# Retention attention into a mixture of experts: first row numbers one step later, places woven, the second expert's rows asked for first

## The chip, the cores and the metric

One core of a Trainium2 chip runs the whole kernel as one program. The metric is the device time of one execution in microseconds (us); a kernel's time is the median of its runs. Engines are called as in the profile: PE (matrix products), DVE and ACT (elementwise work), POOL (elementwise work and indirect DMAs), SP (issues most DMAs).

## The reference

```python
# attention: B=4, H=8, S=768, D=64, blocks of 64 tokens, state kv per (batch, head)
for b in range(12):
    intra = einsum(einsum(qb, kb) * Dmask, vb)
    inter = einsum(qb * lam_pow, kv)
    out[:, :, block b] = intra + inter
    kv = lam_block * kv + einsum(kb * rev_pow, vb)
x = out transposed to [3072, 512]
# mixture of experts, E=8, hidden 1024, each token goes to one expert
e_idx = argmax(x @ w_gate); gate_w = softmax(x @ w_gate)[e_idx]
eom = sigmoid(x @ w_output_gate)
for e in range(8):
    out[mask] = gate_w * eom[:, e] * (relu(x[mask] @ w1[e]) @ w2[e])
```

Only the rows that chose an expert go through its weights, so the kernel has to sort 3072 rows by expert while it runs.

## The kernel before, in words

**Stage 1** computes x in 24 tiles of 128 tokens (tile n is time chunk n // 4 of batch n % 4, all heads). A software pipeline (L1248 to L1334) runs steps s = -2 to 21. A step works on several tiles: `stage_a` transposes keys and queries of tile s+2 on PE into the banks `pk`, `pq` (ACT copies them out); `stage_c1` starts the output `po` of tile s from the state; `stage_b` makes the scores `ps` of tile s+1 and `stage_b2` multiplies them by the decay on DVE (`at`, L407, two halves); `stage_c` finishes `po` of tile s, copies it as `xT`, and adds the new keys to the state (PE `pst`, DVE L464); `stage_d2` (L521) transposes `xT` of an earlier tile on DVE (L530) and stores its rows to DRAM (`x_d`, SP DMA at L532). Tiles 20 to 23 are stored after the loop, two at a time.

PE writes to eight PSUM banks, handed out strictly in turn by `bank`; a step stands when its next bank is still being read.

**Routing.** For each four tiles, PE makes logits (L499, L509), `route_choose` (L542) picks the expert of each row, and `route_place` (L586) gives each row its place in that expert's list: a few small matmuls into a rank bank `pr` (`ranks`) and 15 small DVE operations (L637 to L632, ending in a reciprocal). From tile 8 on they keep their scratch in the rank bank itself, so that bank comes free with the last of the 15. POOL then scatters a record per row into a table in DRAM (`place_scatter`, L677, one indirect DMA per tile). `weave` runs pending small operations between the large ones of a step; `late` holds `ranks` for the next step; `held` holds places for step 21 (`RES + 5`, with `RES0` = 12, `RES` = 16, `LAST` = 20).

At step 12 the expert that leads is picked, to be computed first. At the end of step 15 POOL loads the first numbers of its list (`load_rows`, L831), `row_index` (L861) turns them into row numbers on DVE (L866, four times L871), and POOL gathers x rows from DRAM (`gather`, L897), one indirect DMA for 32 rows of each quarter: the table `work` places these gathers (`row(b)`) and the record scatters (`rec`) at three points of each step. `x_turn` (L908) transposes gathered rows on DVE, `x_hi` (ACT, L928) and `x_lo` (DVE, L932) split them into a high and a low part for the matrix products, which use three products for each pair (L85 to L87). Weights come in pieces of 1 MB over SP (`load_piece`) and are split the same way (ACT L132, DVE L141 and L146).

**Between the loop and the experts** the last tiles are finished while PE already computes the first 192 rows of the first expert with pending `units` (`fill`, `settle`). There `sort_rest` orders the other seven experts, `expert_regs` (L734) reads their numbers into registers of SP and POOL, `load_outs0` loads three tables of places where the results go, `load_rows(1)` the list of the second expert.

**The experts** run in the loop over p (L1437): for each of eight columns fc, `up` makes 12 matmuls into `ph`, ACT makes `hhi` (L1006) and DVE `hlo` (L1007); then the second product, `down`. `next_rows` (L1020) first does a `pace`, a POOL copy of one element of `hhi` that holds POOL until ACT has made it, then gathers for a later expert.

Of the kernel before, what the change touches and what calls it, by code (L numbers as in the profile page):

```python
# [9 lines left out]
F32 = mybir.dt.float32  # L10
# [13 lines left out]
def kernel(  # L24
# [496 lines left out]
    def stage_d2(n, count=1):  # L521
        if count == 1:
            xn = slot(f"xn_{n}")
        else:
            xn = pool.tile([P, 8 * P], F32, tag="wide", bufs=4, name=f"xn_{n}")
        for i in range(count):

            src = live.pop(n + i)["xT"].rearrange("p (g b r) -> p b g r", g=NPAIR, b=4)
            dst = xn[:, i * DM : (i + 1) * DM].rearrange("p (b g c) -> p b g c", b=4, g=NPAIR)
            nc.vector.transpose(dst, src)  # L530
            weave()
        nc.sync.dma_start(  # L532
            x_d[n * P : (n + count) * P, :].rearrange("(i p) m -> p i m", p=P),
            xn[:, 0 : count * DM].rearrange("p (i m) -> p i m", m=DM),
        )
# [196 lines left out]
        )  # L732

    def expert_regs(p, in_i, n):  # L734
        _, regs = nc.values_load_multi_w_load_instructions(
            in_i[0:1, 0:n], engines=[mybir.EngineType.SP, mybir.EngineType.Pool], min_val=0, max_val=E - 1
        )
        expert.update(zip(range(p, p + n), regs))

# [168 lines left out]
    def x_turn(p, i):  # L908
        if p >= E or i >= KT[p]:
            return  # L910
        w = P * (min(4, NB[p] - 4 * i) if p else (4, 2, 4, 1)[i])
        if (p, i // 2) not in ys:
            ys[(p, i // 2)] = pool.tile([P, 8 * P], F32, tag="wide", bufs=4, name=f"y_{p}_{i // 2}")
        nc.vector.transpose(ys[(p, i // 2)][:, 512 * (i % 2) : 512 * (i % 2) + w], xg[(p, i)][:, 0:w])  # L914
# [288 lines left out]
    def settle():  # L1203
        while acts:
            acts.pop(0)()

    def fill(count):
        for _ in range(min(count, len(units))):
            mm, act = units.pop(0)
            mm()  # L1210
            if act:
                acts.append(act)

    with tc.manual_schedule():
# [11 lines left out]
        def row(b):  # L1226
            return lambda: gather(0, b, b + 1, RES0 * P)

        def rec():
# [6 lines left out]
            RES0 + 1: ([], [], [rec]),  # L1236
            RES0 + 2: ([], [rec], [rec]),
            RES0 + 3: ([], [rec], [lambda: load_rows(0, 0, 2, nc.gpsimd)]),
            RES: ([], [], [row(0)]),
            RES + 1: ([], [row(1)], [rec]),  # L1240
            RES + 2: ([rec], [], [rec]),
            RES + 3: ([row(2)], [], [rec]),
            RES + 4: ([row(3)], [], [row(4)]),
            RES + 5: ([row(5)], [], [rec]),
# [3 lines left out]
        for s in range(-2, NTILE - 2):  # L1248
            if s >= 0:
                load_up_to(s + AHEAD - (4 <= s <= RES), 2 if s <= RES else 1)  # L1250
            for i in range(3):
                if s == RES + (2, 4, 5)[i]:
                    load_piece(i)
            if s == -2:
                decay_table()
            if s == 0:
                stage_b(1)
                stage_b2(1)
            rest = stage_a(s + 2)
            if late and s != RES + 5:  # L1260
                late.pop(0)()
            if s >= 1 and s % B == 0:
                logits(s - B, B)
            for f in rest:
                f()
            if s >= 0:
                stage_c1(s)
            stage_a2(s + 2)
            if s == RES + 4:
                stage_q(s + 2)  # L1270
            if s + 1 >= 0 and s != 0:
                stage_b(s + 1)
            if s == RES + 5:
                late.pop(0)()
                seen = rank_counts("plater")
            n = s - 1
            if s >= 1 and s % B == 0:
                logit_rows(s - B)
            if n >= 0 and n % B == B - 1:
                choice = route_choose(n + 1 - B, n + 1)  # L1280
                ranking = route_place(n + 1 - B, n + 1)
                if s != RES + 4:
                    at_once(choice)
                    pace(uncounted[-1][0][0:1, 0, 0:1])
                per_turn[0] = 3 if n >= RES - 1 else 2
            if s + 1 >= 0 and s != 0:
                stage_b2(s + 1)
            stage_k(s + 2)
            if s == RES0 + 1:
                weave(len(later))  # L1290
            if s == RES0 + 2:
                expert_regs(0, order_i, 1)
            if s == RES:
                row_index(0)
            if s == RES + 5:
                for f in held:
                    f()
                keep_places(seen, LATE)
            gap_work(s, "end")
            if s == RES + 1:  # L1300
                weave(len(later))
            if s == RES + 4:
                at_once(choice[:-1])
            if s == RES + 5:
                x_turn(0, 0)
            if 0 <= n < LAST:
                stage_d2(n)
            if s == 0:
                later.extend(inter_tables())
                routing_tables()  # L1310
                order_tables()
            if s == 1:
                weave(len(later))
            if s == 2:
                blank_rows()
            if s >= 0:
                stage_c(s)
            if s == RES + 4:
                choice[-1]()
            if ranking and s == RES + 4:  # L1320
                late.append(ranking[0])
                held = ranking[1:]
                ranking = []
            if ranking and s not in (RES0, RES):
                late.append(ranking[0])
                later.extend(ranking[1:])
                ranking = []
            if ranking:
                first_steps = pick_first() if s == RES0 else []
                for f in first_steps[:1] + ranking:  # L1330
                    f()
                later.extend(first_steps[1:])
                ranking = []
            if s < RES0 - 2:  # L1334
                place_scatter(1)
# [4 lines left out]
        stage_c1(n - 1)  # L1340
        stage_b(n)
        stage_b2(n)
        place_scatter(B)
        load_rows(0, 1, 3, nc.gpsimd)
        x_turn(0, 1)
# [41 lines left out]
            split_hi(2, j)  # L1387
        row_index(0, 1)
        gather(0, 6, 11, LAST * P)
        stage_d2(LAST, 2)  # L1390
        stage_d2(n - 1, 2)
        split_late()
        sort_rest(counts)
        load_outs0()
        expert_regs(1, order_i[:, 1:E], E - 1)
        load_rows(1)
        load_piece(4)
        for h in range(2):
            split_hi(3, 2 * h)
            split_hi(3, 2 * h + 1)  # L1400
            fill(8)
            split_lo2(2, h)
            settle()
        for h in range(2):
            split_lo2(3, h)
            fill(2)
        settle()
        row_index(1)
        gather(1, 0, 4)
        load_piece(5)  # L1410
        x_turn(0, 2)
        x_turn(0, 3)
# [24 lines left out]
        for p in range(E):  # L1437
# [5 lines left out]
            for fc in range(NFC):  # L1443
                if p == 0:
                    up(p, fc, 1)
                    next_rows(1, 6 + fc, 7 + fc, hts[(p, fc)][0][0:1, FIRST : FIRST + 1].bitcast(F32))
                    if fc >= 4:
                        next_split(4, (fc - 4,))
                    if fc >= 5:
                        for f in work[:2]:  # L1450
                            f()
                        work = work[2:]
                else:
                    up(p, fc)
                    next_split(4 * p + 2, (fc,))

                    if fc == 1 and p in TURNED:
                        out_index(p)
                    if fc == 3 and p == 2:
                        count_over()  # L1460
                    if fc >= 4:
                        for f in work[: (fc - 2) // 2]:
                            f()
                        work = work[(fc - 2) // 2 :]
                if fc == 3 and p in TURNED:
                    down_banks(p)
                if p > 0 and fc < 4:
                    b = 4 * 2 if p - 1 in TURNED else 3 * 2 if p > 1 else 2 * 2
                    n = (14 - b + 3) // 4
                    next_rows(p + 1, b + n * fc, b + n * fc + n, hts[(p, fc)][0][0:1, 0:1].bitcast(F32))  # L1470
                if fc == 0:
                    load_outs(p + 1)
                    load_rows(p + 2)
                if p - 1 in TURNED:
                    if fc == 2:
                        fetch_turned(p - 1)
                    if fc >= 5:
                        send_turned(p - 1, fc - 5)
# [127 lines left out]
```

## Time and profile before

| | us |
|---|---|
| median of 3 runs | 435.49 |
| lowest, highest | 432.88, 436.21 |
| the profiled execution | 438.91 |
| its span in the trace | 437.3 |

| engine | busy us | share of the span |
|---|---|---|
| PE | 409.5 | 94% |
| PE weight loads | 372.0 | 85% |
| DVE | 285.1 | 65% |
| POOL | 233.7 | 53% |
| ACT | 189.2 | 43% |

The profile is of one execution, 438.91 us by its own clock and 437.3 us from its first instruction to its last; the shares are averages over stages that differ. PE's clock is granted at one of two levels, 1.2 and 2.4 GHz; the profile shows it as a share of the higher one, 0.98 over the whole span.

### The profile page before, as it was taken

What the parts mean: (1) busy time and instruction counts of PE and PEld (TensorE: products, weight loads), DVE (VectorE), ACT (ScalarE), POOL (GpSimd) and SP (SyncE); (2) the same over time, 40 slices, a digit from 0 to 9 for tenths busy, and PEclk for the clock granted to TensorE, in tenths of its full rate; (3) what the DMA queues carried; (4) which work ended last, traced back from release to release, by engine and by line L of the source; (5) the groups of instructions that cost most, each with busy time, mean ns of one, the idle gap of its engine ahead of it and who ended that gap; (6) DMA issues with size and microseconds to landing.
All of it is one profiled execution on the core that took longest, in us unless ns stands there. A gap on an engine that the chain in (4) does not pass through costs nothing.

```text
span 437.3 us, 10557 instructions
## 1 busy us (share of the span) xinstructions
PE 409.5 (94%) x3869; PEld 372.0 (85%) x3869; DVE 285.1 (65%) x810; ACT 189.2 (43%) x460; POOL 233.7 (53%) x294
## 2 busy tenths in 40 slices
PE   7898999979979997998999999999999999999993
PEld 4787877768859786897999899999999989989983
DVE  3658696756678744773964985796785774874610
ACT  5666655544657113432602533532642552542400
POOL 4176678765854666574468086375476446311011
PEclk9999999996999998999999999999999999999997
DMA  6899988779932491444357455974964886361001
GB/s 169 205 245 250 259 210 225 179 195 233 327 122 85 131 340 43 133 169 133 118 202 238 154 210 163 290 230 148 291 223 122 241 284 214 127 214 47 2 25 49
DMA packets 96077, 79.20 MB, mean 181 GB/s; under 512 B 59452, under 2 KB 71744, under 8 KB 96016
## 3 DMA queue, kind: packets, MB, share of 16 engines
q1 hardware_dynamic: 89696, 65.54, 50.6%
q0 software_dynamic: 6176, 12.90, 9.6%
q8 instruction: 32, 0.52, 0.5%
q14 instruction: 29, 0.24, 0.2%
q10 hardware_dynamic: 144, 0.00, 0.0%
HBM read 62.25 MB, written 16.55 MB: 180 GB/s over the span
## 4 chain that ended last, share of the span: by engine, by line
PE 73%; issue 6%; DMA 6%; DVE 6%; POOL 5%; SPq 2%; ACT 1%; another core or an unknown queue 0%; POOLq 0%; DVEq 0%
PE ph_None L87 8%; PE ph_None L86 8%; PE ph_None L85 8%; PE py L87 5%; PE pyr L86 5%; PE py L86 5%; PE py L85 5%; PE pyr L85 5%; PE pyr L87 5%; PE ps L398 2%; PE ph L86 2%; PE po L439 2%; PE ph L87 2%; PE ph L85 2%; DMA raw<-in_moe_w_dram 1%
## 5 line engine op out<-in xcount | busy, mean ns | idle before, releaser
L897 POOL DMA_INDIRECT xg<-x_d,rows x100 | 110.9, 1109 | 71.6 <-issue 45.2
L1006 ACT ACTIVATE hhi<-ph_None 128x400 fp32r<-128x400 f32 (+4 forms) x56 | 28.0, 501 | 120.0 <-PE ph_None L87 94.5
L86 PE MATMUL ph_None<-xlo,whi 128*128 128x400 f32 (+4 forms) x224 | 76.2, 340 | 1.4 <-issue 1.4
L87 PE MATMUL ph_None<-xhi,wlo 128*128 128x400 f32 (+4 forms) x224 | 76.2, 340 | 1.1 <-issue 1.1
L85 PE MATMUL ph_None<-xhi,whi 128*128 128x400 f32 (+4 forms) x224 | 76.2, 340 | 0.0
L141 DVE TENSOR_TENSOR wlo<-raw,whi 128x512 fp32r<-128x512 f32 x112 | 74.4, 685 | 0.5 <-ACT whi L132 0.5
L132 ACT CAST whi<-raw 128x512 fp32r<-128x512 f32 x128 | 74.6, 616 | 0.0
L1007 DVE SCALAR_TENSOR_TENSOR hlo<-ph_None,hhi 128x400 fp32r<-128x400 f32 (+4 forms) x56 | 31.7, 566 | 47.4 <-ACT hhi L1006 26.9
L87 PE MATMUL py<-hhi,wlo 128*128 128x400 f32 (+2 forms) x128 | 44.6, 349 | 0.1
L86 PE MATMUL py<-hlo,whi 128*128 128x400 f32 (+2 forms) x128 | 44.5, 348 | 0.1
L85 PE MATMUL py<-hhi,whi 128*128 128x400 f32 (+2 forms) x128 | 44.5, 348 | 0.0
L407 DVE TENSOR_TENSOR at<-ps,decay 128x512 f32<-128x512 f32 x48 | 31.1, 682 | 19.5 <-PE ps L398 18.7
L87 PEld LDWEIGHTS ph_None<-xhi,wlo 128*128 128x128 f32 x224 | 42.0, 188 | 1.9 <-issue 1.6
L85 PEld LDWEIGHTS ph_None<-xhi,whi 128*128 128x128 f32 x224 | 42.0, 188 | 1.5 <-issue 1.1
L86 PEld LDWEIGHTS ph_None<-xlo,whi 128*128 128x128 f32 x224 | 42.0, 188 | 0.7 <-issue 0.4
L1123 POOL DMA_INDIRECT out_dram<-yn,table x12 | 12.6, 1053 | 53.3 <-DVE yn L1187 36.0
L343 ACT COPY qT<-pq 64x256 f32<-64x256 f32 x96 | 37.5, 391 | 3.8 <-PE pq L339 2.5
L86 PE MATMUL pyr<-wlo,hhi 128*128 128x512 f32 (+2 forms) x96 | 37.8, 394 | 0.4 <-issue 0.4
L85 PE MATMUL pyr<-whi,hhi 128*128 128x512 f32 (+2 forms) x96 | 37.5, 390 | 0.0
L87 PE MATMUL pyr<-whi,hlo 128*128 128x512 f32 (+2 forms) x96 | 37.4, 390 | 0.0
L677 POOL DMA_INDIRECT tab_d<-rec,idx x24 | 26.5, 1105 | 13.5 <-issue 5.3
L928 ACT CAST xhi<-y 128x256 fp32r<-128x256 f32 (+3 forms) x64 | 19.5, 357 | 31.6 <-DVE y L914 27.2
(214 smaller groups left out, 787.2 us busy)
## 6 DMA issues: line engine op xcount, KB each, us to landing
raw<-in_moe_w_dram SPq DMA_DIRECT2D x32, 1024.0 KB
qkv<-in_k_dram SPq DMA_DIRECT2D x40, 128.0 KB
qkv<-in_q_dram SPq DMA_DIRECT2D x40, 128.0 KB
qkv<-in_v_dram SPq DMA_DIRECT2D x20, 256.0 KB
x_d<-xn SPq DMA_DIRECT2D x20, 256.0 KB
yd<-yo SPq DMA_DIRECT2D x12, 256.0 KB
yr<-yd SPq DMA_DIRECT2D x48, 64.0 KB
xg<-x_d,rows POOLq DMA_INDIRECT x100
```

Of the source, the lines that this page charges most:

```text
L85: nc.tensor.matmul(ps, a[0], b[0], start=first, stop=False)
L86: nc.tensor.matmul(ps, a[0], b[1], start=False, stop=False)
L87: nc.tensor.matmul(ps, a[1], b[0], start=False, stop=last)
L132: nc.scalar.copy(out=hi, in_=src)
L141: eng.tensor_tensor(out=lo, in0=src, in1=hi.bitcast(F32), op=ALU.subtract)
L343: copies = [lambda r=r, view=view, src=src: nc.scalar.copy(out=view(qT[r]), in_=src) for r, view, src in query_parts(pq)]
L407: nc.vector.tensor_tensor(out=at, in0=ps.rearrange("p (g t) -> p g t", g=NPAIR), in1=dec[:, j], op=ALU.mult)
L677: nc.gpsimd.indirect_dma_start(out=tab_d, out_offset=bass.IndirectOffsetOnAxis(ap=idx, axis=0), in_=rec, in_offset=None, bounds_check=P * ...
L897: nc.gpsimd.indirect_dma_start(out=xg[(p, i)][:, m * P : (m + 1) * P], out_offset=None, in_=x_q[0 : 4 * rows], in_offset=bass.IndirectOffs ...
L928: nc.scalar.copy(out=hi, in_=src)
L1006: nc.scalar.activation(out=hi[:, r], in_=ph[:, r], func=AF.Relu)
L1007: nc.vector.scalar_tensor_tensor(out=lo[:, r], in0=ph[:, r], scalar=0.0, in1=hi[:, r].bitcast(F32), op0=ALU.max, op1=ALU.subtract,)
```

## The change

It has seven parts, none of which changes what is computed.

1. The first row numbers (`row_index(0)`) are made at the end of step 17, not 16. The gathers `row(0)` and `row(1)` are a step later, and record scatters are put in their places; one scatter that was inside the loop is now behind it.
2. The places of tiles 12 to 15 are no longer made in one go at the end of step 16: `ranks` goes to step 17, and the 15 DVE operations are woven through it, six in `stage_a2`, three behind each half of `at`, the last three behind the row numbers.
3. At step 21, tile 20 is transposed and stored inside the loop (one SP DMA more); `x_turn(0, 0)` stands ahead of the places of that step, of which six operations stay there and nine go behind the loop's last `at`. After the loop tile 21 is stored alone, tiles 22 and 23 together.
4. The second expert's number is read alone and its list and weight piece 4 are asked for at once; the result tables and the other six numbers follow.
5. Numbers of later experts are read by SP alone, without POOL's registers.
6. The second expert's row numbers and first four gathers stand half a weight split earlier.
7. At p = 1 the gathers for expert 2 are spread: one for each fc (fc 6 has two), each behind its own `pace`, where before fc 0 to 3 had three each.

`live.pop` became `live[...]`, which issues nothing.

```diff
     def expert_regs(p, in_i, n):
+        engines = [mybir.EngineType.SP] + ([] if p else [mybir.EngineType.Pool])
         _, regs = nc.values_load_multi_w_load_instructions(
-            in_i[0:1, 0:n], engines=[mybir.EngineType.SP, mybir.EngineType.Pool], min_val=0, max_val=E - 1
+            in_i[0:1, 0:n], engines=engines, min_val=0, max_val=E - 1
...
-            RES: ([], [], [row(0)]),
-            RES + 1: ([], [row(1)], [rec]),
-            RES + 2: ([rec], [], [rec]),
+            RES + 1: ([], [], [row(0)]),
+            RES + 2: ([row(1)], [rec], [rec]),
...
+            if s == RES + 5:
+                stage_d2(LAST)
             if s + 1 >= 0 and s != 0:
                 stage_b2(s + 1)
...
-            if s == RES:
+            if s == RES + 1:
                 row_index(0)
             if s == RES + 5:
-                for f in held:
+                x_turn(0, 0)
+                for f in held[:6]:
                     f()
                 keep_places(seen, LATE)
...
-            if s == RES + 5:
-                x_turn(0, 0)
...
-            if ranking and s not in (RES0, RES):
+            if ranking and s != RES0:
                 late.append(ranking[0])
                 later.extend(ranking[1:])
                 ranking = []
...
         stage_b2(n)
+        for f in held[6:]:
+            f()
         place_scatter(B)
...
-        stage_d2(LAST, 2)
+        stage_d2(LAST + 1)
         stage_d2(n - 1, 2)
         split_late()
         sort_rest(counts)
-        load_outs0()
-        expert_regs(1, order_i[:, 1:E], E - 1)
+        expert_regs(1, order_i[:, 1:2], 1)
         load_rows(1)
         load_piece(4)
+        load_outs0()
+        expert_regs(2, order_i[:, 2:E], E - 2)
...
             split_lo2(3, h)
             fill(2)
+            if h == 0:
+                row_index(1)
+                gather(1, 0, 4)
         settle()
-        row_index(1)
-        gather(1, 0, 4)
...
-                if p > 0 and fc < 4:
-                    b = 4 * 2 if p - 1 in TURNED else 3 * 2 if p > 1 else 2 * 2
+                if p == 1:
+                    b = 4 + (fc if fc < 6 else 2 * fc - 6)
+                    next_rows(2, b, b + 1 + fc // 6, hts[(p, fc)][0][0:1, 0:1].bitcast(F32))
+                if p > 1 and fc < 4:
+                    b = 4 * 2 if p - 1 in TURNED else 3 * 2
                     n = (14 - b + 3) // 4
```

## Rows read from the trace of the kernel before

**Rows 1.** Busy time by stretch: length, each engine, PEclk, DMA share, GB/s.
```profile
94.00:106.00 12.00, 8.19 (x116) 7.13 (x113) 8.80 (x33) 3.60 (x9) 8.55 (x9) 0.72 0.82 203
...
122.00:130.00 8.00, 5.34 (x84) 4.03 (x81) 6.40 (x16) 4.53 (x14) 5.01 (x4) 1.00 0.19 65
130.00:157.00 27.00, 26.60 (x190) 22.34 (x189) 21.96 (x69) 11.42 (x32) 14.72 (x14) 1.00 0.46 147
157.00:174.00 17.00, 13.80 (x98) 13.15 (x97) 5.13 (x11) 3.91 (x10) 11.96 (x16) 0.90 0.48 158
...
185.00:210.00 25.00, 23.22 (x119) 21.97 (x118) 15.32 (x45) 10.47 (x23) 13.90 (x16) 1.00 0.41 132
...
250.00:430.00 180.00, 180.00 (x982) 171.87 (x980) 118.00 (x290) 69.21 (x154) 81.51 (x89) 1.00 0.55 175
```

**Rows 2.** The chain that ended last, at step 16: start, us, what.
```profile
88.54 4.95 DMA index<-tab_d
```

**Rows 3.** DVE's timeline in steps 16 and 17: start, us, instruction, [idle before, releaser].
```profile
90.53 1.28 DVE L407 TENSOR_TENSOR at<-ps,decay 128x512 f32<-128x512 f32 x2
93.50 0.16 DVE L866 SCALAR_TENSOR_TENSOR rowf<-index 32x8 f32<-32x8 int32 x1 [1.69 <-DMA index<-tab_d]
93.70 0.68 DVE L871 TENSOR_SCALAR rows<-rowf 32x8 int32<-32x8 f32 x4
...
95.78 0.19 DVE L637 TENSOR_TENSOR pr<-pr,ebase 128x32 f32<-128x32 f32 x1
...
98.74 0.18 DVE L632 RECIPROCAL rec<-pr 128x4 f32<-128x4 f32 x1
```

**Rows 4.** PE's timeline in steps 16 to 19, the same columns.
```profile
96.01 0.69 PE L452 MATMUL pst<-qkv,kd 128*64 128x64 f32 x16 [1.48 <-DVE pr L637]
99.03 1.09 PE L339 MATMUL pk<-ident,k 128*128 128x128 f32 x4 [2.33 <-issue]
...
100.90 1.13 PE L422 MATMUL po<-qd,state 64*64 64x128 f32 x16
...
105.81 0.66 PE L339 MATMUL pk<-ident,k 128*128 128x128 f32 x4
...
109.79 0.66 PE L339 MATMUL pk<-ident,qkv 128*128 128x128 f32 x4
```

**Rows 5.** DVE's timeline at the end of the loop.
```profile
117.69 1.29 DVE L407 TENSOR_TENSOR at<-ps,decay 128x512 f32<-128x512 f32 x2 [1.02 <-PE ps L398]
...
122.88 0.71 DVE L914 STREAM_TRANSPOSE y<-xg 128x512 f32<-128x512 f32 x1 [0.21 <-DMA raw<-in_moe_w_dram]
123.51 1.25 DVE L407 TENSOR_TENSOR at<-ps,decay 128x512 f32<-128x512 f32 x2
```

**Rows 6.** ACT's timeline behind the loop.
```profile
125.15 1.11 ACT L928 CAST xhi<-y 128x192 fp32r<-128x192 f32 x4 [4.49 <-DVE at L407]
```

**Rows 7.** PE's timeline behind the loop.
```profile
124.22 1.25 PE L439 MATMUL po<-at,qkv 128*64 128x128 f32 x16 [1.48 <-DVE at L407]
...
128.16 1.06 PE L499 MATMUL pl<-xT,wgs 128*32 128x128 f32 x26 [1.18 <-ACT xT L446]
```

**Rows 8.** DVE's timeline at p = 0, a transposition that waits for its gather.
```profile
183.30 0.45 DVE L914 STREAM_TRANSPOSE y<-xg 128x256 f32<-128x256 f32 x1 [2.57 <-DMA xg<-x_d,rows]
```

**Rows 9.** DMA queues from 152 to 158: packets, MB, share of 16 engines.
```profile
q0 software_dynamic: 17, 0.02, 0.9%
```

**Rows 10.** SP's DMA issues ahead of the experts: start, us to issue, what.
```profile
145.34 1.84 SPq L849 DMA_DIRECT2D table<-tab_d  x3
150.81 0.54 SPq L831 DMA_DIRECT2D index<-tab_d  x1
```

**Rows 11.** The chain that ended last, at p = 1.
```profile
202.96 1.41 issue
```

**Rows 12.** ACT's timeline at p = 0 and p = 1.
```profile
170.45 0.66 ACT L1006 ACTIVATE hhi<-ph 128x256 fp32r<-128x256 f32 x2 [5.33 <-remote]
...
203.04 0.53 ACT L1006 ACTIVATE hhi<-ph_None 128x432 fp32r<-128x432 f32 x1 [6.94 <-PE ph_None L86]
```

More of the change, by code (lines that the diff above doesn't have):

```diff
@@ L526, in stage_d2 @@
         for i in range(count):
-            src = live.pop(n + i)["xT"].rearrange("p (g b r) -> p b g r", g=NPAIR, b=4)
+            src = live[n + i]["xT"].rearrange("p (g b r) -> p b g r", g=NPAIR, b=4)
             dst = xn[:, i * DM : (i + 1) * DM].rearrange("p (b g c) -> p b g c", b=4, g=NPAIR)
```

## The prediction

> **What bounds the kernel.** I began with the busy time by stretch, because the 94% of PE is an average. From 250 to 430 PE is busy for all of 180.00 us, at the full clock [rows 1]: nothing that the change does to transfers or to POOL can shorten that part, it can only be begun earlier. So a gain must come from the four stretches of rows 1 in which PE stands: 94 to 106 (8.19 busy of 12, clock 0.72), 122 to 130 (5.34 of 8), 157 to 174 (13.80 of 17, clock 0.90) and 185 to 210 (23.22 of 25). The reader is to see that the change touches all four. Then I read the chain of waits and each engine's timeline in those stretches, and asked for every stop of PE what ended it.
>
> The profiled execution took 438.91, its span was 437.3; the median is 435.49. I count microseconds off the span and take them off the median; the execution lies 0.8% above it, so a term scales by less than 0.05.
>
> **The places and the first row numbers (parts 1, 2): -4.2.** Before, the index load asked for at 88.54 lands 4.95 later [rows 2]. DVE has finished `at` of tile 17 at 91.8, stands 1.69 for it, makes the row numbers until 94.4, then transposes and updates the state until 95.78, then does 15 places in a run until 98.92 [rows 3]. PE pays twice: 1.48 ahead of `pst` at 96.01, whose bank waits for the state update, and 2.33 ahead of the next transposes at 99.03, whose bank is the rank bank and comes free with the reciprocal [rows 4]. "Issue" stands there as releaser; that the transposes start 0.1 behind the reciprocal is why I read it so. It costs more than 3.8: the next step, from 99.03 to 105.81, takes 6.8, and the one behind it, 105.81 to 109.79, takes 4.0 with the same instructions [rows 4]; the granted clock of 94 to 106 is 0.72 [rows 1], so most of that step ran at the lower of the two levels, 1.2 GHz, behind the two stops. 6.8 - 4.0 = 2.8 more.
>
> After: DVE ends `at` of tile 17 at 91.8 and goes on with the 1.4 us of transposition and update (94.38 to 95.78), until 93.2. Six places at 0.21 each (15 in 3.14) take it to 94.5, the two halves of the next `at` (1.28) with three places behind each to 97.0, the row numbers (0.9) to 97.9, the last three to 98.5. `ranks` now stands behind tile 19's transposes, so the rank bank is needed next by `po` of tile 18. PE no longer stops for `pst`; it runs ahead with transposes until about 96 and then waits for the rank bank until 98.5. That `po` started at 100.90 [rows 4], so 2.4 are won. If the clock then holds, the rest of that step (100.90 to 105.81, 4.9) takes 3.0: transposes of tile 21 at 101.5 instead of 105.81, the sum 4.3; I take 4.2. Bounds: 6.6, if the stop vanishes as well (3.8 + 2.8), and 1.4, if the clock falls again (4.2 - 2.8). The index load has landed by 93.5 and is wanted at 97.0, so DVE waits no more there. Covers: `row(0)` and `row(1)` go out a step later, but the fourth row is wanted only at 122.88 [rows 5]; the scatter that moves behind the loop, a POOL DMA more there, delays only the list load behind it on POOL, for rows that PE takes up after 157. SP stores and loads follow the earlier DVE in the same order.
>
> **The end of the loop (part 3): +0.4.** Tile 20's transposition (0.7, by the row of the same shape) fits DVE's idle 1.02 ahead of 117.69 [rows 5]; its DMA stands on SP ahead of nothing but weight pieces. The last `at` moves ahead of nine places (1.9), so PE's stop of 1.48 at 124.22 goes [rows 7]. But ACT's `xhi` at 125.15 [rows 6], ahead of which stand on DVE the same instructions as before, still holds `xT` and the logits at 128.16 [rows 7]: the 1.48 comes back as a longer stop there. What is new is `x_turn(0, 0)` ahead of the places: it wants its gather some 4 us earlier, with the six places, the last `at`, ACT's `xhi` and PE behind it. Its wait is 0 at best; the nearest prices are 0.21 [rows 5] and 2.57 where a transposition waits for a gather [rows 8]. I take 0.4, near the first, since that is this very transposition in this stretch; bounds 0 and 2.57.
>
> Here a row and a rule part. The row: with SP's weights in the queues (152 to 158), POOL's queue moved 17 packets, 0.9% [rows 9], though three gathers had been issued: gathers come late behind weights. The rule of the Trainium skill, DMA: Bandwidth & Descriptors, section Queues, rings and completion order: each DMA engine takes packets from the queues that have work in turn, so a gather would not stand behind the megabytes of another queue. By the rule the 0.4 falls away and the sum is -5.1; the row decides, and I keep 0.4.
>
> **The second expert's rows first (parts 4 to 6): 0.** SP ends the three table loads at 147.18 and issues the index at 150.81 [rows 10]: 3.6 for seven numbers, some 0.5 each. One number first, tables behind: index and piece 4 are asked for about 5 us earlier. In 130 to 157 PE is busy 26.60 of 27 with the first expert's units [rows 1], so nothing is won there directly: at most 0.4. The row numbers go ahead of half a weight split and may hold DVE, as they did for 1.69 [rows 3], with the split and the next `hlo` queued behind: +1.7 is the upper bound. I take 0, since the index now has the 5 us. POOL's register reads went beside SP's; dropping them saves POOL at most those 3.6, while it waits for row numbers anyway.
>
> **Spread gathers at p = 1 (part 7): -0.9.** PE stops 1.41 at 202.96 [rows 11] and 0.37 more, 1.78 of 185 to 210 [rows 1], when ACT's `hhi` comes 6.94 late [rows 12]. POOL is busy 13.90 of 25 in that stretch and 11.96 of 17 where p = 0 stands, against 81.51 of 180 where PE never does [rows 1]; spreading ten gathers over eight columns thins it. No row shows how gathers hold ACT, so the bounds are 0 and -1.8 and I take the middle. The four added paces hold POOL until `hhi`, with the gathers for expert 3 queued behind; the last gather comes with column 7, and the DVE transposition that wants it may wait the 2.57 of rows 8, which a DVE busy 15.32 of 25 [rows 1] covers.
>
> The stop at p = 0 (3.2 idle and a clock of 0.90 over 17 us, 1.7: together 4.9 [rows 1], with `hhi` 5.33 late [rows 12]) is not addressed. I take 0, bounds -4.9 and +4.9.
>
> **Sum:** -4.2 + 0.4 + 0 - 0.9 = -4.7: 435.49 - 4.7 = **430.8**. One per cent, about what a measurement can tell from no change, is 4.35: the threshold of faster is 431.1, that of slower 439.8.
>
> **The rivals.**
> - *The forecast* (0.44): 430.8, its own range 429.0 to 432.8; just over half of it is faster.
> - *The clock falls again* (0.20). PE still stops once for 2.5 near 98 and, its two waits joined, for about 2.7 near 127. For: it fell behind 1.48 and 2.33 [rows 4]. Against: behind 1.48 and 1.18 [rows 7] it stayed 1.00 [rows 1]. The 2.8 are not won: 433.6. The Trainium skill, TensorE: Matmul & The Clock Gate, Part 1, has the idle array throttled and activity release it; by that rule, too, one stop in place of two leaves it open.
> - *The stop at p = 0 goes as well* (0.18). Weight piece 4 and the gathers for expert 1 are earlier, `hhi` comes in time: of 4.9 some 4 are won: 426.8. For: POOL's run of gathers is where the stop is. Against: no part aims at columns of p = 0.
> - *Slower: gathers in a row* (0.13). Four gathers now start before `settle`, and with POOL's earlier break gone they run on into p = 0's paced ones, and ACT's `hhi` there waits twice as long: +4.9, and p = 1 keeps its 1.8 (+0.9): 436.6; with the clock down as well, 439.4. It decides if POOL in 157 to 174 is busier than 11.96 of 17.
> - *The change doesn't do what it says* (0.05): the places still come in a run, or the index is still late: 435.5.
>
> **The numbers.** Faster: 0.25 of the forecast's 0.44 and 0.18 make 0.43. Slower by over 1%: the worse half of the slower rival, 0.07. The rest, 0.50, is within 1%. The range from 426.5 to 436.8 leaves out the better third of the third case and the worse half of the fourth, with some of the bounds: about 0.2.
>
> **What will show it.** At 96 to 99 PE's timeline should have one stop of about 2.5 ahead of `po`, none ahead of `pst`, and PEclk of 94 to 106 should be near 1.00; tile 21's transposes near 101.5. Around 122 to 130 one stop ahead of the logits, at most 0.5 more idle than the 2.66 before, and `x_turn(0, 0)` waiting under 0.5 for its gather. The index at about 146 and no DVE wait at its row numbers. At p = 1 no "issue" piece above 0.9 in the chain. The forecast is wrong if the clock row stays near 0.7, or if the idle time of 157 to 174 moves by over 2 either way.

## The result and the profile after

The changed kernel takes 432.12 us in the median of 20 runs (429.59 to 437.11), the kernel before, with more runs by now, 436.47: a ratio of 0.9903, 95% interval 0.9877 to 0.9929, or 4.2 us less. A second comparison ("After once more", below) gave 0.988 (0.9831 to 0.9929). The forecast was 430.8, by a gain of 4.7.

Busy time by stretch after the change (columns as in [rows 1]):

```profile
94.00:106.00 12.00, 10.54 (x215) 8.69 (x209) 8.82 (x37) 6.33 (x17) 9.14 (x10) 1.00 0.95 243
...
122.00:130.00 8.00, 5.39 (x54) 3.62 (x52) 5.25 (x16) 4.40 (x13) 4.68 (x4) 0.81 0.23 64
130.00:157.00 27.00, 24.68 (x180) 21.30 (x181) 21.62 (x68) 11.61 (x33) 16.36 (x17) 0.99 0.50 157
157.00:174.00 17.00, 17.00 (x121) 15.47 (x120) 8.39 (x19) 6.76 (x18) 12.72 (x18) 1.00 0.37 122
...
185.00:210.00 25.00, 25.00 (x130) 24.03 (x129) 17.38 (x51) 11.67 (x27) 16.56 (x22) 1.00 0.52 174
```

Against [rows 1] the first stretch has 1.46 of idle PE where it had 3.81, at the full clock, and both stops behind 157 are gone. But 122 to 130 now runs at 0.81, and 130 to 157 has PE idle 2.3 where it was 0.4.

Fixed stretches of the clock mix stages once these have moved. So I cut PE's timeline at the same instructions in each profile: the first matmul of the logits at steps 16 and 20 (L499), of the first expert's units (`ph`, 130.11 before), of its second columns (157.09) and so on to the end of PE's last. Each entry is the difference of two such starts, in us:

| stage | before | before, 2nd profile | after | after, 2nd profile |
|---|---|---|---|---|
| steps 16 to 20 | 24.22 | 22.72 | 20.13 | 22.58 |
| end of the loop, to the first `ph` | 19.30 | 20.59 | 22.83 | 21.13 |
| fill, to p = 0's columns | 26.98 | 27.02 | 28.78 | 29.82 |
| p = 0, columns | 16.96 | 16.61 | 11.50 | 11.51 |
| p = 0, `down`; p = 1, both | 50.89 | 48.52 | 48.51 | 48.51 |
| p = 2, both | 37.85 | 37.19 | 37.36 | 36.66 |
| p = 3 to 7 | 167.27 | 167.25 | 167.28 | 167.24 |

The table is the result in short. The steps won 4.1 in the first pair, as forecast, and 0.1 in the second; the end of the loop lost 3.5 and 0.5; the fill lost 1.8 and 2.8; p = 0 won 5.5 and 5.1, which stood in no term; p = 1 won 2.4 and nothing. From p = 3 on nothing moves, as [rows 1] said.

PE's timeline in steps 17 to 19 after the change (columns as in [rows 4]):

```profile
97.15 0.90 PE L422 MATMUL po<-qd,state 64*64 64x128 f32 x16
99.15 1.10 PE L398 MATMUL ps<-qT,kT 64*64 64x128 f32 x32 [1.10 <-DVE rec L632]
...
101.67 0.65 PE L339 MATMUL pk<-ident,k 128*128 128x128 f32 x4
...
104.88 0.30 PE L398 MATMUL ps<-qT,kT 64*64 64x128 f32 x1 [0.31 <-issue]
...
106.91 0.66 PE L339 MATMUL pk<-ident,qkv 128*128 128x128 f32 x4
```

This answers to [rows 4]: one stop of 1.10 for the reciprocal in place of 1.48 and 2.33, and the step behind it at the full clock. Tile 21's transposes start 4.1 earlier although this execution was 1.1 later at 91, so 5.2 are won up to them. But tile 22's follow 5.2 behind them, where 4.0 was the step's length before: PE stops in the middle of `ps`, and the profile names no releaser. The obvious suspect is POOL (start, us, what):

```profile
100.86 1.02 POOL xg L898
...
101.91 0.76 POOL qd L373
...
102.83 1.06 POOL tab_d L677
...
105.22 0.73 POOL qd L373
```

The gather `row(1)` and two scatters, moved into step 18, stand there between the halves of `qd`. But they are not the cause. In the profile with twelve more gathers at p = 4 (below), which is the changed kernel up to there, POOL starts this gather, the first scatter and the later `qd` at the same distances from the step's start (-0.8, 1.2 and 3.5), and the step takes 4.0:

```profile
103.91 0.66 PE L339 MATMUL pk<-ident,k 128*128 128x128 f32 x4
...
107.89 0.66 PE L339 MATMUL pk<-ident,qkv 128*128 128x128 f32 x4
```

The end of the loop on DVE, then on PE (as [rows 5] and [rows 7]):

```profile
115.29 1.29 DVE L407 TENSOR_TENSOR at<-ps,decay 128x512 f32<-128x512 f32 x2 [1.06 <-PE plater L726]
...
118.17 0.71 DVE L915 STREAM_TRANSPOSE y<-xg 128x512 f32<-128x512 f32 x1 [1.59 <-issue]
...
120.67 1.28 DVE L407 TENSOR_TENSOR at<-ps,decay 128x512 f32<-128x512 f32 x2
...
123.52 0.42 DVE L915 STREAM_TRANSPOSE y<-xg 128x256 f32<-128x256 f32 x1
```

```profile
121.41 1.25 PE L439 MATMUL po<-at,qkv 128*64 128x128 f32 x16 [1.75 <-DVE at L407]
...
125.41 0.41 PE L499 MATMUL pl<-xT,wgs 128*32 128x128 f32 x2 [1.38 <-ACT xT L446]
126.99 1.92 PE L499 MATMUL pl<-xT,wgs 128*32 128x128 f32 x26 [1.18 <-ACT xT L446]
```

`x_turn(0, 0)` stands 1.59 where it stood 0.21 [rows 5]; the row names no releaser, but the fourth gather, which it needs, had gone out at 111.69. The stop that was to go, 1.48 [rows 7], is 1.75; a third one has come; and from the last start to the first `ph` PE takes 3.77 (126.99 to 130.76) where it took 1.95 (128.16 to 130.11), at half the clock for most of it: 1.8 lost behind the stops.

The fill, on ACT and on PE:

```profile
148.56 0.33 ACT L1007 ACTIVATE hhi<-ph 128x192 fp32r<-128x192 f32 x1 [4.72 <-remote]
```

```profile
150.47 0.50 PE L86 MATMUL pyr<-wlo,hhi 128*128 128x512 f32 x1 [1.55 <-DVE wlo L146]
```

### The profile page after: what moved, and what is told of

It is laid out like the page before. It is cut to its first block, busy times and chain, and to the rows that moved or that the text cites. A ratio compares the mean times of both kernels' runs of the same rounds, so it can differ in the third digit from the quotient of the medians.

```text
span 430.4 us, 10574 instructions
## 1 busy us (share of the span) xinstructions
PE 407.1 (95%) x3869; PEld 369.7 (86%) x3869; DVE 284.9 (66%) x810; ACT 189.5 (44%) x460; POOL 236.0 (55%) x299
## 4 chain that ended last, share of the span: by engine, by line
PE 68%; DVE 10%; DMA 6%; POOL 5%; issue 5%; SPq 3%; another core or an unknown queue 1%; ACT 1%; POOLq 0%; DVEq 0%; ACTq 0%
PE ph_None L87 8%; PE ph_None L85 8%; PE ph_None L86 8%; PE pyr L86 5%; PE pyr L87 5%; PE pyr L85 5%; PE py L87 4%; PE py L85 4%; PE py L86 4%; PE ps L398 3%; POOL xg L898 2%; DMA xg<-x_d,rows 2%; PE po L439 2%; DVE at L407 2%; DMA qkv<-in_q_dram 2%
## 5 line engine op out<-in xcount | busy, mean ns | idle before, releaser
L898 POOL DMA_INDIRECT xg<-x_d,rows x100 | 112.3, 1123 | 63.7 <-issue 35.9
```

The costliest lines, as they stand in the source:

```text
L898: nc.gpsimd.indirect_dma_start(out=xg[(p, i)][:, m * P : (m + 1) * P], out_offset=None, in_=x_q[0 : 4 * rows], in_offset=bass.IndirectOffs ...
```

## The experiments

A first theory, from the table: parts 1 and 2 are worth 4, part 3 costs 3 to 4, parts 4 to 6 trade the stop at p = 0 against some of the fill, part 7 removes the stop at p = 1. The rivals: the sum of the prediction term by term, and stops that come and go by themselves. The first four versions ran on one chip, where the kernel before took 437.45.

**Parts 1 and 2 undone.**

```diff
+            RES: ([], [], [row(0)]),
+            RES + 1: ([], [row(1)], [rec]),
+            RES + 2: ([rec], [], [rec]),
...
-            if s == RES + 1:
+            if s == RES:
                 row_index(0)
...
-            if ranking and s != RES0:
+            if ranking and s not in (RES0, RES):
```

> The changed kernel without parts 1 and 2 (row numbers at step 16, places in one go at its end), all else as changed. Both traces: tile 21's transposes move from 101.67 back to about 106, the two stops of PE near 96 and 99 return, PEclk of 94 to 106 falls to about 0.7; 432.1 + 4.1 = 436.2, no faster than before. Rival: the later stages absorb the shift, since their DMAs do not move with PE; then 434 or less.

Measured: 0.9984 (0.9955 to 1.0013), against 0.9903 with them: 3.5 us by the two ratios. Both stops are back:

```profile
96.72 0.69 PE L452 MATMUL pst<-qkv,kd 128*64 128x64 f32 x16 [2.04 <-DVE pr L637]
99.73 1.09 PE L339 MATMUL pk<-ident,k 128*128 128x128 f32 x4 [2.33 <-issue]
```

The steps take 24.25. The 3.5 are theirs, a little under the 4.1 expected; the rival falls. The other five parts alone gain 0.7 (by the interval, from 2.0 to a loss of 0.6).

**Part 3 undone** (tile 20 stored after the loop, all 15 places ahead of the last `at`, `x_turn(0, 0)` behind them).

```diff
-            if s == RES + 5:
-                stage_d2(LAST)
...
-                x_turn(0, 0)
-                for f in held[:6]:
+                for f in held:
                     f()
                 keep_places(seen, LATE)
...
+            if s == RES + 5:
+                x_turn(0, 0)
...
-        for f in held[6:]:
-            f()
...
-        stage_d2(LAST + 1)
+        stage_d2(LAST, 2)
```

> The changed kernel with the end of the loop as before (part 3 undone). The prediction's working (+0.4 for part 3): 431.7. What the trace after shows (a wait of 1.59 for the gather, two stops ahead of the logits and the clock down for some 1.8 us, 3.7 lost between tile 23's transposes and the first expert's matmuls): 428.5 to 430.5, PEclk of 122 to 130 at 1.00.

Measured: 430.31, ratio 0.9821 (0.9776 to 0.9866). Against 0.9903 for the changed kernel that is 3.6 us less, against its second comparison (0.988) 2.6, and against the next two versions, which keep part 3 and ran beside this one (0.9861, 0.9869), about 2. So part 3 costs some 2 to 3.6 us. The profile shows less of it: the end of the loop takes 21.46, against 22.83, 23.06 and 20.90 in the changed kernel and those two. PE's stops are 2.00, 0.39 and 0.95, the clock of 122 to 130 is 0.84 and not the 1.00 expected, and the wait has only moved, from `x_turn(0, 0)` to `x_turn(0, 1)`:

```profile
118.58 0.71 DVE L915 STREAM_TRANSPOSE y<-xg 128x512 f32<-128x512 f32 x1 [0.21 <-DMA raw<-in_moe_w_dram]
...
122.08 0.45 DVE L915 STREAM_TRANSPOSE y<-xg 128x256 f32<-128x256 f32 x1 [1.61 <-issue]
```

**Parts 4 to 6 undone.**

```diff
-        engines = [mybir.EngineType.SP] + ([] if p else [mybir.EngineType.Pool])
+        engines = [mybir.EngineType.SP, mybir.EngineType.Pool]
...
-        expert_regs(1, order_i[:, 1:2], 1)
+        load_outs0()
+        expert_regs(1, order_i[:, 1:E], E - 1)
         load_rows(1)
         load_piece(4)
-        load_outs0()
-        expert_regs(2, order_i[:, 2:E], E - 2)
...
-            if h == 0:
-                row_index(1)
-                gather(1, 0, 4)
         settle()
+        row_index(1)
+        gather(1, 0, 4)
```

> The changed kernel without parts 4 to 6 (tables and seven numbers ahead of the second expert's index, row numbers and four gathers behind the weight splits, registers on POOL too). The prediction's working (0): 432.1. If these parts are what removed the stop at p = 0 (5.5 us between the traces) and cost 1.8 in the fill: about 435.8, with idle PE at p = 0's columns. If the stop at p = 0 comes and goes by itself: about 430.3.

Measured: 0.9861 (0.9817 to 0.9905): no loss from undoing them. In its profile p = 0's columns take 13.22 (11.50 with the parts) and the fill 29.51 (28.78). The fill's stop is not part 6's doing; without it, it is longer:

```profile
151.95 0.50 PE L86 MATMUL pyr<-wlo,hhi 128*128 128x512 f32 x1 [3.23 <-DVE wlo L146]
```

**Part 7 undone** (three gathers behind each of four columns at p = 1).

```diff
-                if p == 1:
-                    b = 4 + (fc if fc < 6 else 2 * fc - 6)
-                    next_rows(2, b, b + 1 + fc // 6, ...)
-                if p > 1 and fc < 4:
-                    b = 4 * 2 if p - 1 in TURNED else 3 * 2
+                if p > 0 and fc < 4:
+                    b = 4 * 2 if p - 1 in TURNED else 3 * 2 if p > 1 else 2 * 2
```

> The changed kernel with three gathers behind each of four columns at p = 1 as before (part 7 undone). The prediction's working (0.9): 433.0. The traces (the up product of p = 1 took 20.9 before, 18.8 after): 434.2, with ACT's hhi some 6 us late at columns 4 and 5 and PE stopping 1.4 to 1.8 there. Rival: that stop is not of the gathers; then 432.1 and no stop.

Measured: 0.9869 (0.9829 to 0.9908), no loss in time. In its profile p = 1's columns take 19.97 instead of 18.80, and `hhi` is late; first without part 7, then the same columns of the changed kernel:

```profile
194.94 0.53 ACT L1007 ACTIVATE hhi<-ph_None 128x432 fp32r<-128x432 f32 x1 [3.61 <-PE ph_None L87]
...
200.75 0.54 ACT L1007 ACTIVATE hhi<-ph_None 128x432 fp32r<-128x432 f32 x1 [4.77 <-PE ph_None L87]
```

```profile
193.90 0.53 ACT L1007 ACTIVATE hhi<-ph_None 128x432 fp32r<-128x432 f32 x1 [1.31 <-PE ph_None L87]
196.25 0.53 ACT L1007 ACTIVATE hhi<-ph_None 128x432 fp32r<-128x432 f32 x1 [1.31 <-PE ph_None L87]
```

The size, 1.2, is near the 0.9 forecast, but as a part of the time it is not shown.

Up to p = 1 this is the changed kernel, and two of its stages differ all the same. The fill takes 32.09 and p = 0's columns 11.52, together 43.61 against 40.28 (before: 43.94). And at the end of the loop nearly the same stops leave the clock at 1.00 from 122 to 130:

```profile
120.89 1.26 PE L439 MATMUL po<-at,qkv 128*64 128x128 f32 x16 [1.64 <-DVE at L407]
...
124.89 0.41 PE L499 MATMUL pl<-xT,wgs 128*32 128x128 f32 x2 [1.38 <-ACT xT L446]
126.48 1.06 PE L499 MATMUL pl<-xT,wgs 128*32 128x128 f32 x26 [1.18 <-ACT xT L446]
```

The next four ran on another chip, where the kernel before took 429.03.

**Another order at the end of the loop.** `x_turn(0, 0)` behind the six places, the nine others behind `x_lo`:

```diff
-                x_turn(0, 0)
                 for f in held[:6]:
                     f()
                 keep_places(seen, LATE)
+                x_turn(0, 0)
...
-        for f in held[6:]:
-            f()
-        place_scatter(B)
-        load_rows(0, 1, 3, nc.gpsimd)
         x_turn(0, 1)
         # x_hi, x_lo
+        for f in held[6:]:
+            f()
+        place_scatter(B)
+        load_rows(0, 1, 3, nc.gpsimd)
```

> The changed kernel with another order at the end of the loop: x_turn(0, 0) behind the six places instead of ahead of them, and the nine places left over behind x_turn(0, 1), x_hi and x_lo instead of ahead of them; tile 20 is still stored in the loop. Theory: part 3 lost its time twice on DVE, 1.6 by the wait for the gather ahead of the last at, and 1.9 by nine places ahead of x_turn(0, 1), xhi and so xT and the logits; then the stops ahead of the logits shrink to under 1, the clock of 122 to 130 stays at 1.00, and the time is 3 to 4.5 less than the changed kernel's: ratio to before 0.980 to 0.983. Rival: the loss is the store of tile 20 and its transposition inside the loop; then no gain, 0.990.

Measured: 0.9967 (0.9933 to 1.0), a miss. DVE got to `x_turn(0, 1)` early and stood there, and PE with it:

```profile
120.22 0.45 DVE L915 STREAM_TRANSPOSE y<-xg 128x256 f32<-128x256 f32 x1 [4.77 <-DMA xg<-x_d,rows]
```

```profile
122.12 0.41 PE L499 MATMUL pl<-xT,wgs 128*32 128x128 f32 x2 [4.19 <-ACT xT L446]
```

So DVE's order was only half of the cause: the last gather, issued at 111.85, is usable at 120.2. Its queue moves next to nothing for the first half of that time (112 to 116, packets, MB, share):

```profile
q1 hardware_dynamic: 665, 0.96, 89.8%
q0 software_dynamic: 14, 0.02, 1.6%
```

**Part 3 undone, and the gathers spread at p = 2 and 3.**

```diff
+                if p in (2, 3):
+                    b = (4 * 2 if p - 1 in TURNED else 3 * 2) + fc
+                    next_rows(p + 1, b, b + 1, ...)
-                if p > 1 and fc < 4:
+                if p > 3 and fc < 4:
```

> The changed kernel without part 3, and with the gathers at p = 2 and 3 spread too (one behind each hhi, in place of two or three behind the first four). Theory: runs of indirect DMAs on POOL without breaks make ACT's hhi late; at p = 2 it was 3 to 5 us late at columns 3 to 5 in every kernel so far, and here it should be under 0.2 late there. PE stood only 0.3 to 0.7 for it, so the time is the one of e2_no_part_3 (0.982) or up to 0.5 less. Rival: the lateness at p = 2 has another cause (weights, tables, buffers); then it stays at 3 to 5.

Measured: 0.9919 (0.989 to 0.9948), not the 0.982 expected. No `hhi` is late at p = 2, but at p = 2 none is in any of the four profiles on this chip, so the run cannot test the spreading.

**Parts 1 and 2 alone, on the kernel before.**

> The kernel before with parts 1 and 2 alone. Both traces: 3.5 to 4.2 less than before, ratio 0.990 to 0.992, and the stop at p = 1 of 0.9 to 1.8 still there. If the rest of the change without part 3 is worth nothing: the ratio of e2_no_part_3, 0.982. Rival: without the earlier index of the second expert the 4 us are given back at p = 0; then 0.997 or more.

Measured: 0.9947 (0.9912 to 0.9982), 2.3 us, less than expected. The steps take 21.30 in its profile, where PE waits for a load of v:

```profile
104.51 1.09 PE L439 MATMUL po<-at,v 128*64 128x128 f32 x16 [2.36 <-DMA v<-in_v_dram]
```

With the old gathers of parts 4 to 7, p = 0's columns take 11.51 and p = 1's 19.12: the large stops of [rows 1] are missing on this chip without the change.

**Twelve more gathers at p = 4.**

> The changed kernel with twelve more indirect DMAs on POOL at p = 4, three behind each of its columns 0 to 3, of 32 bytes a row into a spare tile that nothing reads (result unchanged). Theory: ACT's hhi at p = 4, at most 0.5 late so far, becomes 3 to 6 us late at columns 3 to 6, and PE stops there. Rival: hhi's lateness does not come from POOL; then p = 4 is as before.

Measured: 428.05 in one run; the columns of p = 4 are on time:

```profile
298.28 0.51 ACT L1007 ACTIVATE hhi<-ph_None 128x400 fp32r<-128x400 f32 x1 [1.10 <-issue]
300.44 0.51 ACT L1007 ACTIVATE hhi<-ph_None 128x400 fp32r<-128x400 f32 x1 [1.15 <-PE ph_None L87]
```

So a run of indirect DMAs on POOL is not enough to make `hhi` late on this chip, where no profile shows the large stops at p = 0 and p = 1; what it would do on the other two is not shown. It is also the only time of the changed kernel on this chip, with the gathers added: 0.998 of the kernel before, by one run, so what the change gains where these stops are missing is not settled.

The last four ran on a third chip, where the kernel before took 436.83.

**Before once more.**

> The kernel before once more, unchanged, for a second profile. In the last comparison the kernel before took 429.0 in place of 436 to 437, and in four profiles ACT's hhi was never late. If that lateness belongs to the chip and not to the kernel: where before takes about 429 here, no hhi is over 1 us late and the stops at p = 0 (3.2) and p = 1 (1.8) are missing; where it takes about 437, they are there. If it belongs to the kernel: they are there at either time.

```profile
157.00:174.00 17.00, 14.75 (x100) 13.54 (x98) 5.57 (x11) 3.91 (x10) 12.37 (x16) 0.90 0.50 163
185.00:210.00 25.00, 25.00 (x130) 24.03 (x129) 18.72 (x54) 11.95 (x26) 15.68 (x17) 1.00 0.48 154
```

The stop at p = 0 is there, nearly to the size of [rows 1]; that of p = 1 is missing, with the same three gathers behind each column. The first was there in both profiles of this kernel on such chips, the second in one of the two.

**After once more.**

> The changed kernel once more, unchanged, to have it beside the others on one chip. On a chip where before takes 436 to 437: ratio 0.990. On one where it takes 429: there part 7 has no stop to remove and parts 4 to 6 none to shorten, parts 1 and 2 alone gave 0.9947 there, and part 3 costs 1.5 to 3.5: ratio 0.997 to 1.003.

Measured: 430.66, ratio 0.988. Its column in the table ("after, 2nd profile") shows p = 0 on time again. `x_turn(0, 0)` waits 1.61, and the steps have a wait of 1.10 for v with the low clock behind it, which ate the gain there:

```profile
105.33 1.97 PE L439 MATMUL po<-at,v 128*64 128x128 f32 x16 [1.10 <-DMA v<-in_v_dram]
```

**Rows a step earlier**, in the order of "Another order at the end of the loop".

```diff
-            RES + 2: ([row(1)], [rec], [rec]),
-            RES + 3: ([row(2)], [], [rec]),
-            RES + 4: ([row(3)], [], [row(4)]),
-            RES + 5: ([row(5)], [], [rec]),
+            RES + 2: ([row(1)], [], [row(2)]),
+            RES + 3: ([row(3)], [], [row(4)]),
+            RES + 4: ([row(5)], [rec], [rec]),
+            RES + 5: ([rec], [], [rec]),
```

> e5_loop_end_order with the gathers of the first expert's rows 2 to 5 a step earlier (two in each of steps 18 and 19, the last in 20) and the record scatters behind them. There DVE stood 4.77 for the last gather ahead of x_turn(0, 1), with xhi, xT and PE's logits behind it (PE idle 4.19 and 1.18, the clock down behind it). Theory: the end of the loop is bounded by the landing of the last gather, asked for at step 21 behind saturated queues; then that wait falls under 1, PE's two stops shrink to under 1.5 together, and the ratio is 4 to 7 us below that of e5_loop_end_order (0.980 to 0.987). Rival: the gathers wait for bytes and land no earlier, or PE meets the loads of v as at 101 and 104 before; then 0.992 or more.

Measured: 0.9873 (0.9806 to 0.9941), on another chip than the order it amends. PE's two stops are 0.48 and 1.17 (1.65 together, where under 1.5 was expected), `x_turn(0, 0)` waits 0.21 and `x_turn(0, 1)` not at all, and the end of the loop takes 19.53 (21.13 in the changed kernel's profile beside it).

**The same, tile 20 stored after the loop, gathers spread at p = 2 and 3.**

> e11_rows_a_step_earlier with tile 20 stored after the loop as before, and the gathers at p = 2 and 3 spread. If the store of tile 20 inside the loop costs by its 256 KB ahead of the gathers and its 0.6 on DVE: 0.5 to 1.5 less than e11. If not, the same as e11; the spreading matters (0.5 to 1) only where hhi comes late.

Measured: 427.37, ratio 0.9817 (0.9764 to 0.987). DVE no longer waits for the last gather:

```profile
116.32 0.71 DVE L915 STREAM_TRANSPOSE y<-xg 128x512 f32<-128x512 f32 x1 [0.21 <-DMA x_d<-xn]
116.95 1.25 DVE L407 TENSOR_TENSOR at<-ps,decay 128x512 f32<-128x512 f32 x2
118.13 0.42 DVE L915 STREAM_TRANSPOSE y<-xg 128x256 f32<-128x256 f32 x1
```

The steps take 19.22 and the end of the loop 19.41, 5.1 less together than in the changed kernel's profile on this chip; 2.0 of it are given back in the fill and at p = 0 (43.30 against 41.33), where PE now comes before what it needs. At p = 2, without and with the spreading, on one chip:

```profile
231.91 0.52 ACT L1007 ACTIVATE hhi<-ph_None 128x416 fp32r<-128x416 f32 x1 [3.30 <-PE ph_None L87]
```

```profile
226.76 0.52 ACT L1007 ACTIVATE hhi<-ph_None 128x416 fp32r<-128x416 f32 x1 [1.17 <-PE ph_None L87]
```

The lateness goes, and p = 2 takes 35.84 instead of 37.35. The end of the loop is where it was (19.53 in the version before), so storing tile 20 inside the loop is not what cost there. This version is below the changed kernel beside it (430.66), and the change without part 3 below the versions beside it that keep part 3.

## Why the prediction was right

The gain was forecast as 4.7 and is 4.2. One term carries it: without parts 1 and 2 the other five gave 0.7. That this is near the 0.5 forecast for them is luck, for inside it part 3 cost more than was forecast, and p = 0 won what stood in no term. By its own sign the prediction failed there: it was to be wrong "if the idle time of 157 to 174 moves by over 2 either way", and that fell from 3.2 to nothing. Undoing the other parts one at a time does not show what made up for part 3.

**Parts 1 and 2, -4.2: right in size.** 4.1 in the first pair of profiles, 3.5 by the runs with and without. Inside, two misses cancel in the first pair. The stop was 1.10 instead of 2.5, since the bank that waits is taken by `ps`, not by `po`: so 5.2 were won up to tile 21's transposes. Behind them step 18 lost 1.2, in stops whose cause stays open (POOL's order is not it). In two other profiles PE met the loads of v there (1.10 and 2.36). "SP stores and loads follow the earlier DVE in the same order" was not enough: with the DMA engines busy for 0.90 and 0.88 of 94 to 106 in those two, the loads did not come as much earlier as PE did. On the other chip parts 1 and 2 alone gave 2.3; whether the load of v is why, no run separates.

**Part 3, +0.4: wrong, it cost some 2 to 3.6.** The step that failed is "I take 0.4, near the first, since that is this very transposition in this stretch". The wait was 1.59 and 1.61, and 1.51 to 1.91 in the three other profiles with parts 1 to 3 as changed, inside the bounds of 0 and 2.57 and nearer to the far one: the 0.21 [rows 5] was measured behind 15 places that gave the gather 4 us to land. Moving the transposition took the cover away, and the row that showed a small wait showed the cover. Asking for the gathers a step earlier, with six places ahead again, took the wait down to 0.21. The stop that should have gone stayed (1.75; 2.00 without part 3, and 1.48 and 2.08 in the two profiles of before), and PE's three stops are 4.31 together against 3.34 without part 3: that is 1.0 of the cost. The clock is less certain: it fell behind these stops, as the second rival had it for this place, and 1.8 by the rows were lost before the first `ph`, but behind 1.64, 1.38 and 1.18 it stayed at 1.00, and without part 3 it fell too. The profiles do not place the rest of the 2 to 3.6. The row also decided rightly against the rule of the Trainium skill (DMA: Bandwidth & Descriptors, Queues, rings and completion order), by which the gather would not stand behind the weights: with the loop's end in another order it took 8.4 us from issue to use, with 89.8% of the engines' time on SP's queue in 112 to 116, against 2.2 where no weights moved (last section).

**Parts 4 to 6, 0: right in time, wrong inside.** The runs show no loss from undoing them. But the fill lost 1.8 and 2.8, and not by a wait of the row numbers, which found their index landed: `hhi` came 4.3 behind its matmuls (ACT idle 4.72), `hlo` and the weight split queue behind it on DVE, and PE behind that. p = 0 won 5.5 and 5.1. That is the third rival's stop: it had 4 for it, and fill and p = 0 together gave 3.7 and 2.3. Parts 4 to 6 are only a piece of it: with them undone the columns still took 13.22, not 16.96. Nor is the sum steady, for without part 7, which acts later, fill and p = 0 took as long as before. What removed the stop at p = 0 stays open.

**Part 7, -0.9: right where the stop is.** 1.2 in one pair; in the second profile of before there was nothing to win. The "6.94 late" of the prediction is ACT's idle time; behind its matmuls `hhi` came 6.2 late there, and 7.4 late at p = 0 where the prediction has 5.33.

The fourth rival fell: POOL was busier at p = 0 (12.72 of 17 against 11.96), the point from which it should have decided, and PE stood less.

**What stays open** is why `hhi` comes late. On two chips it does where POOL runs gather after gather. At p = 1 it came 5.9 and 6.2 late in two of three profiles without the spreading, and at most 1.4 in the seven with it; at p = 2 it came 3.1 to 5.2 late in all nine profiles without, and under 1 in the one with it. On a third chip, with the same gathers and with twelve more, neither is seen. Runs of gathers are a condition there and not the whole cause. Weights or code on the DMA queues are not it: from 163.5 to 174 before, while PE stood, POOL's queue alone moved anything.

## What to carry to other kernels

A wait that the trace shows as small may be small because of the work ahead of it: before that work is moved, look up when the transfer was asked for and when it landed. Where the queues are nearly full, as here (0.88 to 0.95), a faster engine may meet its loads, so bring the requests forward first and reorder the consumer second. And a sum that comes out right proves none of its terms: cut both timelines at the same instructions and check stage by stage.

## What was not expected of the hardware

The same kernel takes 436 to 437 us in three comparisons and 429.03 in a fourth, on another chip. Where it takes longer, the profiles show ACT's `hhi` at p = 0 up to 7 us behind the last of its column's 12 matmuls (at 170.45 where PE had them done by 163.0, in the profile before). On the faster chip it comes on time, and with parts 1 and 2 alone p = 0's columns take 11.51 there instead of 16.96 and 16.61: most of the difference. With the lateness PE halts between single matmuls, at steps of 0.7 to 1.4 us (0.70, 0.92, 0.33, 0.45 and 0.80 idle from 166 to 170.4 before).

An indirect DMA took 8.4 us from issue to use beside SP's weights, and only 1.6% of the engines' time went to its queue in the first half of that. Where no weights moved, the gather issued at 167.80 before had its data moved between 169.4 and 170, 2.2 us after its issue (packets, MB, share):

```profile
q0 software_dynamic: 28, 0.07, 40.7%
```
